# Talking-heads attention and gated convolution block: even chunks, wide first loads transposed by TensorE, first product a chunk later

## The chip, the cores and the metric

One core of one Trainium2 chip runs the whole program in one launch. The metric is the device time of a run in microseconds (us), as the median of a few runs; lower is better.

## The reference, cut to what matters

Four batches, 12 heads, 448 positions, 64 numbers a head, everything in fp32. Attention mixes its heads twice, before and after the softmax; a feed-forward block with a convolution over positions follows.

```
scores = 0.125 * q @ k.T                            # [4, 12, 448, 448]
scores = einsum('bhij,hg->bgij', scores, w_pre)     # heads mixed
attn   = softmax(scores)                            # exp(s - max) / (sum + 1e-9)
attn   = einsum('bhij,hg->bgij', attn, w_post)      # heads mixed again
x      = (attn @ v), heads side by side             # [4, 448, 768]
h      = relu(x @ w_in)                             # [4, 448, 1024]
c      = conv_w[0]*h[s-1] + conv_w[1]*h[s] + conv_w[2]*h[s+1]
out    = (h * sigmoid(c)) @ w_out                   # [4, 448, 768]
```

The weights of the feed-forward block come as 64-bit floats; the kernel loads them as pairs of 32-bit words and puts fp32 numbers together on the chip ("decoding": one ACT, one POOL and three DVE steps for a piece of 128x256).

## The kernel before, in words

The query rows of a batch are cut into tiles of 10 rows, and the tiles into four chunks: 9, 12, 12 and 12 tiles in batch 0, and 12, 12, 12 and 9 in the others (`TILES`, L27), so 16 chunks in all, numbered 0 to 15 here. A chunk goes through these steps:

- `qk` (L602): scores of two heads at a time, all rows of the chunk (90 or 120) against the 448 keys. A call is four matmuls on quarters of the array: for each of the two heads the first 64 rows and then the rest, 56 rows where the chunk has 120 and 26 where it has 90. Two copies (`qk_out`, ACT and DVE) bring the two heads from PSUM to SBUF. In chunk 0 the calls take turns between two PSUM pools, later all go through the two buffers of `ps_q`.
- `relayout` (L629): one DMA a head writes these rows into `mt`, where the 12 heads of one row lie on neighbouring partitions. There are two `mt` tiles, for odd and even chunks.
- `premix` (L638), a pair of tiles at a time: the first head mix on PE. Then row maximum (DVE), exponential with its sum (ACT), 1/sum (POOL, DVE), scaling of the second mix's weights by it (DVE), `postmix` (L685) on PE, whose result is already transposed (keys on partitions), and two copies to SBUF (`post_out`, ACT and DVE).
- `av` (L729): attention times v, two heads a call, six calls a chunk, and a copy into `x` (`av_out`).
- `mm1` (L780), per batch and 128 of the 1024 columns: x times w_in, six matmuls over the full array, then `relu` and a store to a scratch tensor in DRAM. For batches 0 to 2 two of these products stand in each chunk of the next batch; those of batch 3 come behind the last chunk.

In the end h is loaded again, convolved, gated and split in two parts (DVE, ACT), and `mm2` multiplies it by w_out in 672 matmuls.

The scores need q and k with their 64 numbers on partitions. Batch 0's keys and the queries of chunks 0 and 1 are loaded with rows on partitions (`load_k0`, `load_q0`) and transposed on PE with an identity matrix (`tr_k0`, `tr_q0`), then copied. All later queries and keys come in quarters: four DMAs of 32 partitions for one chunk's queries (`load_q`, L581) or for the keys of two heads (`load_k`, L567), and DVE transposes blocks of 32x32 (`tr_q`, `tr_k`). v of two heads comes in three DMAs in runs of 64 numbers, and POOL clears the rest of the last block.

The order of all instructions is fixed when the program is built: `plan` (L161) gives each operation an engine, a cost and a due time from a table `P` of numbers, and the class `Order` puts them in one list; each engine works through its part of it in order. Nearly all DMAs are issued by SP, in that order too: one whose data or buffer is not ready holds up those behind it.

Of the kernel before, what the change touches and what calls it, by code (L numbers as in the profile page):

```python
# [25 lines left out]
R, HR = 10, 5  # L26
TILES = [(9, 12, 12, 12)] + 3 * [(12, 12, 12, 9)]  # L27
# [18 lines left out]
T0, T1 = TILES[0][:2]  # L46
RH = R * (T0 + T1) // 2
ST_X = 6
N_PIECES = N_IN + FC * 3

P = dict(
    pm=-2.097, mx=-1.044, ex=-1.09, ep=-2.124, rc=0.122, wn=1.958, po=1.009, ev=0.636, qk=0.649, st=3.01,
    rl=-8.601, lead=6.642, av=2.442, ao=-0.878, a0=-3.11, q1w=0.882, q1s=-3.0, cw=1.318, vl=6.611, nq=5.578,
    nqs=-4.33, tq=14.316, ahead=17.24, tk=2.322, tks=0.913, nk=7.795, dec=14.624, dwi=3.76, dwo=5.594,
    wo0=108.805, look=0.033, step=2.1, busy0=5, k0a=-9.826, k0d=-0.402, m1=3.894, m1w=5.94, tail=4.022,
# [5 lines left out]
QUEUES = 8  # L61


class Order:


    def __init__(self):
        self.ops, self.done = {}, {}
# [5 lines left out]
    def run(self, free, look):  # L74
# [21 lines left out]
        rings, landed = [0.0] * 16, [0.0] * QUEUES  # L96
        shape = 1
        for _ in range(len(ops)):
# [19 lines left out]
            if isinstance(cost, tuple):  # L118
# [6 lines left out]
                end += .9  # L125
# [14 lines left out]
def q_rows(c):  # L140
    b, i0, T = CHUNKS[c]
    r0 = min(i0, S - 128) if c > 1 else i0
    return b, r0, i0 - r0
# [17 lines left out]
def plan(P):  # L161

    od = Order()

    def add(due, engine, cost, *key, after=(), ahead=None):
        od.add(due, engine, cost, *key, after=after, since=22 + (due - (ahead or P["ahead"])) * P["step"])
# [7 lines left out]
    for g in range(3):  # L174
        add(-11 + g, "PE", .55, "tr_q0", g, after=[("load_q0", g)])
        for c in range(2):
            add(-10.8 + g + 2 * c, ("DVE", "ACT")[c], (.3, .35)[c], "out_q0", g, c, after=[("tr_q0", g)])
    for p in range(NP):
        n = P["k0a"] + P["k0d"] * p
        add(n, "PE", .6, "tr_k0", p, after=[("load_k0", p), ("out_k0", p - 3)])  # L180
        add(n, ("ACT", "DVE")[p % 2], .5, "out_k0", p, after=[("tr_k0", p)])
# [3 lines left out]
    for c in range(NCH):  # L185
        if c >= 4:
            turns += [("mm1", c // 4 - 1, 2 * (c % 4) + i) for i in range(2)]
        turns += [("av", c, 0), ("av", c, 3)]

    order = []  # L190
    for x in turns:
        order.append(x)
    before = {}
    for x, y in zip(order, order[1:]):
        before[y] = ("relu", *x[1:]) if x[0] == "mm1" else ("av_out", *x[1:])
# [9 lines left out]
    for c in range(NCH):  # L205
# [33 lines left out]
        for h in range(H):  # L239
            n = sp - P["lead"] + h * w if c > 1 else P["q1s"] + P["q1w"] * h if c else -8.6 + .3 * h  # L240
            i = c * H + h
            free_s = [("qk_out", *divmod(i - 2 - j, H)) for j in range(2)]
            free_st = [("relayout", *slot_of[i])] if i in slot_of else []
            free_mt = [("premix", *pairs[number[c - 1, 0] - 1])] if h == 1 and c > 1 else []
            if h % 2:
                ops = [("tr_k", b, h // 2)] if b else [("out_k0", h // 2)]
                ops += [("tr_q", c, h // 6 * 3)] if c > 1 else [("out_q0", h // 4, c)]
                if c == 0:
                    ops += [("out_q0", g, 1) for g in range(min(h // 2 + 1, 3))]
                    free_s = [("qk_out", 0, h - 4 - j) for j in range(2)]  # L250
# [27 lines left out]
    for b in range(B):  # L278
        s0 = start_of(4 * b - 2)
        for p in range(NP):  # L280
            n = BASE[4 * b] + 1 + 2 * p + P["vl"] if b else 2.5 + p
            ready = [("av", 4 * b - 1, p)] if b else [("qk_out", 1, 5), ("relayout", 1, p)]
            for i in range(3):
                add(n + .1 * i, "SP", (.6, 16, .6) if i < 2 else (.4, 16, .2), "load_v1", b, p, i, after=ready)
            add(n, "POOL", .15, "zero_v", b, p, after=ready)
            add(n, "POOL", .0, "load_v", b, p, after=[("load_v1", b, p, i) for i in range(3)] + [("zero_v", b, p)])
            i = NP * b + p
            if b:
                n = s0 + P["tk"] + P["tks"] * (p - 2)
# [41 lines left out]
    for f in range(FC):  # L331
        if f < 3:
            free = [("premix", 14, len(PAIRS[14]) - 1)]
        elif f < 7:
            free = [("premix", last, len(PAIRS[last]) - 1)]
        else:
            free = [("tr_k", B - 1, NP - 1)]
# [42 lines left out]
    for g in range(3):  # L380
        od.done["load_q0", g] = 3.2 + 2.1 * g, "SP"
    for p in range(NP):
        od.done["load_k0", p] = 3.8 + .7 * p + .7 * (p // 2), "SP"
    order = od.run(dict(PE=4.0, ACT=4.2, DVE=2.0, POOL=9.0, SP=4.6), P["look"])
# [4 lines left out]
def tile_talking_heads_conv_glu(  # L389
# [48 lines left out]
    warm = const.tile([128, 1], F32, name="warm")  # L438
    wi = const.tile([128, KC, FF], U32, name="wi")
# [64 lines left out]
    def identity():  # L504
        nat["id"] = st_p.tile([128, 128], F32, tag="st", name="ident")
        make_identity(nc, nat["id"])

    def prepare():
# [434 lines left out]
```

## Time and profile before

| | us |
|---|---|
| median of 3 runs | 688.12 (685.66 to 689.55) |
| the profiled execution's own time | 690.48 |
| its span, first to last instruction | 688.7 |
| PE busy | 659.7 (96%) |
| DVE busy | 412.0 (60%) |
| ACT busy | 343.2 (50%) |

The mean granted TensorE clock is 0.977 of full speed. A record of PE includes time in which its matmul waits for others on the array, so the busy share of PE says little about how well it is used; what a piece of work takes is read from the start of one group of matmuls to the start of the next. A call of `qk` or a pair of tiles in `premix` shows as 8 records (each fp32 matmul is two), a pair of tiles in `postmix` as 64, three calls of `av` as 48, one `mm1` product as 12.

### The profile page before, as it was taken

To read this page: it belongs to the slowest core of one execution; us is meant where nothing else is said; L and a number is where in the kernel's file an instruction comes from. 1 tells how busy PE (TensorE), PEld (TensorE's weight loads), DVE (VectorE), ACT (ScalarE), POOL (GpSimd) and SP (SyncE) were. 2 spreads that over 40 slices of the span, in tenths; PEclk is the share of its full clock that TensorE was granted. 3 is DMA by queue.
4 is the path that set the end of the run, shared out by engine and by line. 5 is a ranking of instruction groups with operands and counts; after the bars stand their busy time and mean duration, and the time that the engine had idled before them with its cause. 6 is when DMAs were issued, how large, how long until landed. Compare 5 with 4: busy or idle time off the path is not lost.

```text
span 688.7 us, 23692 instructions
## 1 busy us (share of the span) xinstructions
PE 659.7 (96%) x9981; PEld 425.9 (62%) x9981; DVE 412.0 (60%) x974; ACT 343.2 (50%) x808; POOL 75.1 (11%) x186
## 2 busy tenths in 40 slices
PE   8899969799989999999999999999999999999997
PEld 6145646465635555645464655654565559999997
DVE  2467676775555666647474656644654399999100
ACT  3267645655545565646455565645634254434100
POOL 4000001231020220201100111101101000000000
PEclk9889988989999999999999999999999999999999
DMA  7766688878877658586755655632423443443111
GB/s 150 200 149 184 172 192 203 209 182 180 196 181 212 160 171 217 151 185 185 170 143 161 163 167 149 190 117 85 152 79 132 123 136 118 127 128 112 56 47 46
DMA packets 90348, 104.64 MB, mean 152 GB/s; under 512 B 32514, under 2 KB 79106, under 8 KB 90242
## 3 DMA queue, kind: packets, MB, share of 16 engines
q1 hardware_dynamic: 88846, 102.02, 55.3%
q8 instruction: 78, 1.28, 0.8%
q10 hardware_dynamic: 1299, 1.10, 0.6%
q14 instruction: 29, 0.23, 0.1%
q0 software_dynamic: 96, 0.01, 0.0%
HBM read 48.23 MB, written 15.99 MB: 93 GB/s over the span
## 4 chain that ended last, share of the span: by engine, by line
PE 85%; DMA 6%; ACT 3%; DVE 3%; issue 2%; SPq 1%; POOL 0%; ACTq 0%; DVEq 0%
PE h L784 21%; PE o L878 17%; PE s L614 14%; PE t L695 11%; PE a L736 10%; PE m L651 10%; DMA nq<-in_q_dram 2%; ACT e L664 1%; DMA nk<-in_k_dram 1%; DMA v<-in_v_dram 1%; DMA raw<-in_moe_w_in_dram 1%; PE tk L542 1%; ACT at L460 1%; DVE nm L656 1%; DVE mq L594 1%
## 5 line engine op out<-in xcount | busy, mean ns | idle before, releaser
L784 PE MATMUL h<-x,wi 128*128 128x448 f32 x384 | 159.1, 555 | 0.0
L664 ACT ACTIVATE e<-m,nm 124x448 f32<-124x448 f32 x180 | 114.9, 639 | 75.1 <-DVE nm L656 37.4
L656 DVE TENSOR_REDUCE nm<-m 124x1 f32<-124x448 f32 x180 | 106.4, 615 | 52.0 <-PE m L651 51.3
L695 PEld LDWEIGHTS t<-wn,e 60*64 60x64 f32 x5760 | 106.5, 137 | 47.8 <-issue 28.6
L614 PE MATMUL s<-mk,mq 64*64 64x448 f32 (+2 forms) x768 | 126.5, 577 | 7.4 <-ACT st L460 2.6
L460 ACT COPY st<-s 120x448 f32<-120x448 f32 (+1 forms) x161 | 82.1, 536 | 79.4 <-PE s L614 32.6
L878 PE MATMUL o<-wo,g 128*128 128x384 f32 x672 | 117.4, 337 | 0.0
L878 PEld LDWEIGHTS o<-wo,g 128*128 128x128 f32 x672 | 116.9, 188 | 0.4 <-DVE g L863 0.2
L695 PE MATMUL t<-wn,e 60*64 60x60 f32 x5760 | 110.6, 221 | 5.7 <-DVE at L462 2.4
L784 PEld LDWEIGHTS h<-x,wi 128*128 128x128 f32 x384 | 69.2, 191 | 75.0 <-issue 63.7
L651 PE MATMUL m<-mt,wpre 64*64 64x448 f32 (+1 forms) x704 | 96.5, 568 | 6.4 <-ACT e L664 3.0
L736 PEld LDWEIGHTS a<-at,v 128*64 128x64 f32 x1536 | 75.9, 139 | 22.9 <-issue 6.4
L736 PE MATMUL a<-at,v 128*64 128x120 f32 (+1 forms) x1536 | 86.3, 266 | 2.9 <-DVE at L462 0.9
L462 DVE COPY at<-t 128x480 f32<-128x480 f32 (+1 forms) x92 | 61.2, 666 | 31.8 <-PE t L695 31.4
L614 PEld LDWEIGHTS s<-mk,mq 64*64 64x64 f32 (+2 forms) x768 | 28.0, 131 | 63.3 <-issue 32.7
L460 ACT COPY at<-t 128x480 f32<-128x480 f32 (+1 forms) x92 | 57.9, 630 | 8.8 <-PE t L695 8.6
L670 POOL TENSOR_SCALAR sm<-sm 124x2 f32<-124x2 f32 (+1 forms) x92 | 21.4, 233 | 314.0 <-ACT e L664 308.0
L651 PEld LDWEIGHTS m<-mt,wpre 64*64 64x64 f32 (+1 forms) x704 | 25.3, 134 | 44.6 <-issue 30.3
L847 DVE SCALAR_TENSOR_TENSOR cv<-hpad,cws,cv 128x448 f32<-128x448 f32 x64 | 42.8, 678 | 0.1
L789 ACT ACTIVATE hs<-h 128x448 f32<-128x448 f32 x32 | 17.3, 542 | 47.5 <-PE h L784 34.5
L682 DVE TENSOR_SCALAR wn<-wpost,rs 124x60 f32<-124x60 f32 x180 | 37.0, 248 | 1.2
L664 ACT ACTIVATION_READ_ACCUMULATOR e<-m,nm 124x1 f32 x180 | 36.5, 203 | 0.0
(68 smaller groups left out, 377.8 us busy)
## 6 DMA issues: line engine op xcount, KB each, us to landing
mt<-st SPq DMA_DIRECT2D x120, 210.0 KB
nq<-in_q_dram SPq DMA_DIRECT2D x56, 168.0 KB
nk<-in_k_dram SPq DMA_DIRECT2D x72, 108.0 KB
mt<-st SPq DMA_DIRECT2D x48, 157.5 KB
h<-hs SPq DMA_DIRECT2D x32, 224.0 KB
hpad<-h SPq DMA_DIRECT2D x32, 224.0 KB
raw<-in_moe_w_in_dram SPq DMA_DIRECT2D x24, 256.0 KB
raw<-in_moe_w_out_dram SPq DMA_DIRECT2D x24, 256.0 KB
```

The source lines that it names most:

```text
L460: nc.scalar.copy(out=out, in_=in_)
L462: nc.vector.tensor_copy(out=out, in_=in_)
L614: nc.tensor.matmul(out=pqs[c, h - 1 + i][m:e], lhsT=qops[c][s, p, o + m:o + e], rhs=kops[b, p][s], start=True, stop=True)
L651: nc.tensor.matmul(out=pms[c, some[i]][64 * s:64 * s + 64], lhsT=wpre[rows, i], rhs=mt[rows, some[s]], start=True, stop=True)
L656: nc.vector.tensor_reduce(out=nm[0:PN], in_=pms[c, t][0:PN], axis=AX.X, op=ALU.max, negate=True)
L664: nc.scalar.activation(out=e[0:PN], in_=pms.pop((c, t))[0:PN], func=AF.Exp, bias=nm[0:PN], accum_out=sums[c, t // 2][0:PN, t % 2:t % 2 + 1])
L682: nc.vector.tensor_scalar(out=wns[c, k][0:PN, i], in0=wpost[0:PN], scalar1=rs[0:PN, i:i + 1], scalar2=None, op0=ALU.mult)
L695: nc.tensor.matmul(out=pts[c, k][s][64 * half:64 * half + 64, i, j], lhsT=e[rows, o:o + 64], rhs=wn[rows, i], start=True, stop=True)
L736: nc.tensor.matmul(out=pas[c][64 * hh:64 * hh + 64, p % 3, 0:n], lhsT=vts[b, p][:, hh, j, :], rhs=ats[c][:, j, 2 * p + hh, 0:n], start=(j ...
L784: nc.tensor.matmul(out=phs[b, f], lhsT=wi[:, kk, f * 128:(f + 1) * 128].bitcast(F32), rhs=xs[b][:, kk], start=(kk == 0), stop=(kk == KC - 1))
L847: nc.vector.scalar_tensor_tensor(out=cv, in0=hp[:, t:S + t], scalar=w, in1=cv, op0=ALU.mult, op1=ALU.add)
L878: nc.tensor.matmul(out=pos[r, o], lhsT=g, rhs=w, start=(f == 0 and j == 0), stop=(f == FC - 1 and j == 2))
```

## The change

1. The chunks of batch 0 have 10, 11, 12 and 12 tiles, those of the others 12, 12, 11 and 10. The number of tiles, of pairs of tiles and of `qk` calls stays.
2. Queries of chunks 0 to 7 are loaded with rows on partitions, in two DMAs of six heads a chunk (`q_load`), transposed on PE (`q_tr`, 12 matmuls for six heads) and copied by DVE or ACT (`q_out`). Keys of batches 0 and 1 go the same way (`k_load`, `k_tr`, `k_out`; 8 matmuls for two heads). The later ones take the old way. From chunk 2 and batch 1 on, these transposes use the two PSUM buffers of `qk`.
3. In batches 0 and 1 the keys stay in the order in which they were loaded (four neighbouring keys on a partition), so `k_out` copies straight, v of two heads is loaded in the same order by one DMA, `postmix` makes blocks of 64 and 48 keys, and `av` works on 112 partitions.
4. `mm1` of batches 0 and 1 stands one chunk later; batch 2's products are spread 3, 3 and 2 over the last three chunks.
5. At the start q of chunk 0 is loaded in two parts, keys between them; six of the 12 relayouts of chunk 0 are issued by ACT, and the clearing of `mt` by POOL instead of SP.
6. The numbers of the table `P` are others, and the order follows them.

```diff
-TILES = [(9, 12, 12, 12)] + 3 * [(12, 12, 12, 9)]
+TILES = [(10, 11, 12, 12)] + 3 * [(12, 12, 11, 10)]
+MM1_AT = [[4 * b + 5 + f // 2 for f in range(FC)] for b in range(B - 2)] + [[13, 13, 13, 14, 14, 14, 15, 15]]
+K_PE, Q_PE = 2, 8
...
-    nqs=-4.33, tq=14.316, ahead=17.24, tk=2.322, tks=0.913, nk=7.795, dec=14.624, dwi=3.76, dwo=5.594,
+    dec=15.218, dwi=5.977, dwo=5.863, wo0=107.878, look=0.04, step=0.16, step1=2.488, la=15.81, busy0=5,
...
+    def k_load(b, p, eng=nc.sync):
+        nat["k", b, p] = nat["k0"][:, p] if b == 0 else nk_p.tile([112, 2, JC, D], F32, tag="nk", name="nkr")
+        eng.dma_start(out=nat["k", b, p].rearrange("j h c d -> j h (c d)"),
+                      in_=k[b, 2 * p:2 * p + 2].rearrange("h (j c) d -> j h (c d)", c=JC))
+    def k_tr(b, p):
+        pl, tag = (ps_q, "s") if b else (ps_t, "t") if p % 3 < 2 else (ps_a, "a")
...
+    def k_out(b, p):
+        kops[b, p] = ko_p.tile([128, S], F32, tag="mk", name="mk")
+        copy_of(("ACT", "DVE")[p % 2], kops[b, p].rearrange("p (c j) -> p c j", c=JC), trs.pop(("k", b, p)))
+    def q_load(c, g, eng=nc.sync):
...
+        s = slice(6 * g, 6 * g + 6)
+        eng.dma_start(out=nat["q", c][:, s].rearrange("j n u d -> j n (u d)"),
+                      in_=q[b, s, r0:r0 + 128].rearrange("n (j u) d -> j n (u d)", u=2))
+    def q_tr(c, g):
+        pl, tag = (ps_m, "m") if c < 2 else (ps_q, "s")
+        ps = pl.tile([128, 3, 2, 64], F32, tag=tag, name="tq")
+        for p in range(3):
+            i = 6 * g + 2 * p
             for u in range(2):
                 for hh in range(2):
+                    nc.tensor.matmul(out=ps[64 * hh:64 * hh + 64, p, u], lhsT=nat["q", c][:, i + hh, u],
+                                     rhs=ident[0:64, 0:64], start=True, stop=True)
...
-        nc.sync.dma_start(out=nat["mt"][c % 2][4 + h:124:12, 0:T, :], in_=sts.pop((c, h))[0:R * T])
+        (nc.sync if c or h % 2 else nc.scalar).dma_start(out=nat["mt"][c % 2][4 + h:124:12, 0:T, :], in_=sts.pop((c, h))[0:R * T])
...
+    def blocks(c):
+        return 112 if CHUNKS[c][0] < K_PE else 128
...
-                o = min(128 * j + 64 * half, S - 64)
+                m = blocks(c) - 64 if half else 64
+                o = min(blocks(c) * j + 64 * half, S - m)
...
-        if i < 2:
+        if b < K_PE:
+            nc.sync.dma_start(out=vts[b, p][0:112].rearrange("j h c d -> j h (c d)"),
+                              in_=v[b, 2 * p:2 * p + 2].rearrange("h (j c) d -> j h (c d)", c=JC))
+        elif i < 2:
```

The first place is the start of PE's list. `tq` and `tk` are transposes of queries and keys, `s` are the scores (`qk`), `m` the first head mix. Before, from the second group of key transposes on:

```order
L542 MATMUL tk_256<-ident,nk_140 64x112 x8
L555 MATMUL tq_268<-ident,nq_141 64x105 x8
L542 MATMUL tk_279<-ident,nk_140 64x112 x8
L614 MATMUL s<-mk,mq 64x448 x2
L614 MATMUL s<-mk,mq 26x448 x2
L614 MATMUL s<-mk,mq 64x448 x2
L614 MATMUL s<-mk,mq 26x448 x2
```

And the changed program from its first transposes on:

```order
L613 MATMUL tq<-ident,nqr 64x64 x24
L587 MATMUL tk<-ident,nk_140 64x112 x16
L670 MATMUL s<-mk,mq 64x448 x2
L670 MATMUL s<-mk,mq 36x448 x2
L670 MATMUL s<-mk,mq 64x448 x2
L670 MATMUL s<-mk,mq 36x448 x2
L587 MATMUL tk<-ident,nk_140 64x112 x24
L670 MATMUL s<-mk,mq 64x448 x2
L670 MATMUL s<-mk,mq 36x448 x2
```

The rest of a chunk's rows is 36 (later 46 or 56) wide where it was 26. Ahead of the first `m` there are now nine calls of `qk`, four `q_tr` and six `k_tr`; before there were eleven calls, three `tr_q0` and six `tr_k0`.

The second place is SP's list of DMAs around the keys of batch 1 (`nk`, `nkr`); `mt` are relayouts, `raw` pieces of w_in, `nq`, `nqr` queries. Before:

```order
L586 DMA nq<-in_q_dram 32x6x224
L631 DMA mt<-stx 10x12x448 x2
L572 DMA nk<-in_k_dram 32x864 x4
L631 DMA mt<-stx 10x12x448
L765 DMA raw<-in_moe_w_in_dram 128x512
L572 DMA nk<-in_k_dram 32x864 x4
L631 DMA mt<-st 10x12x448
L586 DMA nq<-in_q_dram 32x6x224
L572 DMA nk<-in_k_dram 32x864 x4
L631 DMA mt<-st 10x12x448 x2
L765 DMA raw<-in_moe_w_in_dram 128x512
L572 DMA nk<-in_k_dram 32x864 x4
```

Changed, where the keys of batch 1 begin:

```order
L603 DMA nqr<-in_q_dram 64x6x128 x2
L578 DMA nkr<-in_k_dram 112x2x256 x2
L687 DMA mt<-stx 10x11x448 x2
L687 DMA mt<-stx 10x12x448 x3
L687 DMA mt<-st 10x12x448 x3
L830 DMA raw<-in_moe_w_in_dram 128x512 x3
L687 DMA mt<-stx 10x12x448 x4
L603 DMA nqr<-in_q_dram 64x6x128 x2
L687 DMA mt<-stx 10x12x448 x2
L830 DMA raw<-in_moe_w_in_dram 128x512 x2
L687 DMA mt<-st 10x12x448 x2
L578 DMA nkr<-in_k_dram 112x2x256
```

The keys of batch 1 began among the relayouts of chunk 3 and now begin at the end of those of chunk 1; two heads take one DMA instead of four, and a chunk's queries two instead of four.

## Rows read from the trace of the kernel before

**Rows 1.** Windows, seven stages: busy us (and instructions) of each engine, clock, DMA
```profile
0.00:35.38 35.38, 29.65 (x238) 13.99 (x242) 11.89 (x20) 10.56 (x18) 7.27 (x24) 0.91 0.72 176
35.38:73.62 38.24, 35.98 (x822) 20.13 (x814) 25.78 (x70) 28.06 (x73) 3.24 (x15) 0.95 0.67 163
73.62:142.83 69.21, 58.30 (x1306) 39.24 (x1304) 47.20 (x117) 37.40 (x94) 10.80 (x23) 0.88 0.84 198
142.83:173.10 30.27, 29.17 (x555) 16.09 (x553) 21.49 (x56) 18.59 (x48) 6.57 (x15) 1.00 0.76 179
173.10:270.07 96.97, 94.37 (x1583) 52.34 (x1583) 59.60 (x150) 53.57 (x133) 14.03 (x28) 0.98 0.71 186
270.07:532.00 261.93, 259.15 (x4721) 149.21 (x4721) 150.73 (x379) 146.29 (x357) 32.33 (x80) 1.00 0.54 151
532.00:688.70 156.70, 153.10 (x768) 134.94 (x768) 95.36 (x182) 48.74 (x89) 0.85 (x1) 1.00 0.31 98
```

**Rows 2.** Chain of waits, 78 to 100 us: start, us, what
```profile
78.75 2.93 DMA raw<-in_moe_w_in_dram
...
83.41 7.79 DMA nk<-in_k_dram
...
91.21 1.05 SPq L572
...
93.21 6.10 DMA nq<-in_q_dram
```

**Rows 3.** Timeline, 332 to 335 us, a call of `qk` on 90 rows
```profile
333.01 1.79 PE L614 MATMUL s<-mk,mq 64*64 64x448 f32 x8
...
333.87 0.13 PEld L614 LDWEIGHTS s<-mk,mq 64*26 64x26 f32 x4 [0.71 <-issue]
...
334.74 0.64 PE L784 MATMUL h<-x,wi 128*128 128x448 f32 x1
```

**Rows 4.** Timeline of PE, 275 to 277 us, a call of `qk` on 120 rows
```profile
275.27 0.93 PE L614 MATMUL s<-mk,mq 64*64 64x448 f32 x8
276.13 1.77 PE L784 MATMUL h<-x,wi 128*128 128x448 f32 x4
```

**Rows 5.** Groups by form, PE: mean ns of one record
```profile
L614 PE MATMUL s<-mk,mq 64*26 64x448 f32 x96 | 22.5, 545 | 0.0
```

**Rows 6.** Timeline of PE, 327 to 351 us: starts give the length of each piece
```profile
327.33 4.78 PE L784 MATMUL h<-x,wi 128*128 128x448 f32 x12
332.04 1.16 PE L695 MATMUL t<-wn,e 60*64 60x60 f32 x64
...
343.44 0.98 PE L651 MATMUL m<-mt,wpre 64*64 64x448 f32 x8
344.25 1.11 PE L695 MATMUL t<-wn,e 60*64 60x60 f32 x64
345.18 1.79 PE L614 MATMUL s<-mk,mq 64*64 64x448 f32 x8
...
347.81 2.68 PE L736 MATMUL a<-at,v 128*64 128x120 f32 x48
350.42 1.16 PE L695 MATMUL t<-wn,e 60*64 60x60 f32 x64
```

**Rows 7.** Chain of waits, 5 to 36 us, the start
```profile
5.23 1.67 PE tq L555 x16
...
9.21 0.72 PE tq L555 x16
...
11.70 2.45 PE tk L542 x48
...
15.64 8.88 PE s L614 x40
...
28.77 1.97 PE s L614 x6
30.73 0.52 ACT stx L460
```

More of the change, by code (lines that the diff above doesn't have):

```diff
@@ L89, in release @@
                     t = max(t, end + (LAG[e] if e != engine or e in ("SP", "DVE") else 0))
+                    if e == "SP" and engine != "SP" and "load" in k[0]:
+                        t = max(t, end + LAG[e] + self.late)
             ready[engine].append((due, i, t, key))
@@ L161, in plan, with add @@
 def plan(P):
-    od = Order()
-    def add(due, engine, cost, *key, after=(), ahead=None):
-        od.add(due, engine, cost, *key, after=after, since=22 + (due - (ahead or P["ahead"])) * P["step"])
+    od = Order(P["late"])
+    def add(due, engine, cost, *key, after=()):
+        x = due - (P["la"] if "load" in key[0] else P["ahead"])
+        od.add(due, engine, cost, *key, after=after, since=22 + P["step"] * min(x, 45) + P["step1"] * max(0, x - 45))
     last = NCH - 1
@@ L172, in plan, with k_ready, q_ready @@
     place = {x: i for i, x in enumerate(tiles)}
[L174 to L177, printed above, removed]
+    def k_ready(b, p):
+        return ("k_out" if b < K_PE else "tr_k", b, p)
+    def q_ready(c, h):
+        return ("q_out", c, h // 6) if c < Q_PE else ("tr_q", c, h // 6 * 3)
+    for c in range(2):
+        for g in range(2):
+            n = -11 + 2 * g if c == 0 else P["q1p"] + .3 * g
+            add(n, "PE", .55, "q_tr", c, g, after=[("q_load", c, g)] + [("k_tr", 0, 5)] * c)
+            add(n, ("DVE", "ACT")[g], .47, "q_out", c, g, after=[("q_tr", c, g)])
@@ L184, in plan @@
+    for x in seq:
+        if x[0] == "qk" and x[1] == 0 and x[2] % 4 == 3:
+            continue
+        outs = [("qk_out", x[1], x[2] - 1), ("qk_out", x[1], x[2])] if x[0] == "qk" else [(x[0][0] + "_out", *x[1:])]
+        free_s[x] = []
+        for o in outs:
+            free_s[x] += [banks[n_s % 2]] if n_s > 1 else []
+            banks[n_s % 2] = o
+            n_s += 1
+    for x, y in zip(seq, seq[1:]):
+        prev_s[y] = x
     turns = []
     for c in range(NCH):
-        if c >= 4:
-            turns += [("mm1", c // 4 - 1, 2 * (c % 4) + i) for i in range(2)]
+        turns += [("mm1", b, f) for b in range(B - 1) for f in range(FC) if MM1_AT[b][f] == c]
@@ L188, in plan @@
         turns += [("av", c, 0), ("av", c, 3)]
-    order = []
-    for x in turns:
-        order.append(x)
     before = {}
-    for x, y in zip(order, order[1:]):
+    for x, y in zip(turns, turns[1:]):
         before[y] = ("relu", *x[1:]) if x[0] == "mm1" else ("av_out", *x[1:])
@@ L378, in plan @@
         add(end + 14 + 4 * r + 6, "SP", (.4, 16, 1.0), "store", r, after=[("mm2_out", r, o) for o in range(2)])
[L380 to L384, printed above, removed]
+    for i, x in enumerate([("q_load", 0, 0)] + [("k_load", 0, p) for p in range(3)] + [("q_load", 0, 1)] + [
+            ("k_load", 0, p) for p in range(3, NP)] + [("q_load", 1, g) for g in range(2)]):
+        od.done[x] = 5.2 + i * .95, "SP"
+    order = od.run(dict(PE=4.0, ACT=4.2, DVE=2.0, POOL=10.0, SP=5.0), P["look"])
     return order, od
@@ L549, in tr_q0 @@
-    def tr_q0(g):
-        ps = ps_m.tile([128, 2, 2, RH], F32, tag="m", name="tq0")
-        for p in range(2):
-            i = 4 * g + 2 * p
+                nc.tensor.matmul(out=trs["k", b, p][64 * hh:64 * hh + 64, c], lhsT=x[:, hh, c],
+                                 rhs=ident[0:112, 0:112], start=True, stop=True)
+    def k_out(b, p):
+        kops[b, p] = ko_p.tile([128, S], F32, tag="mk", name="mk")
+        copy_of(("ACT", "DVE")[p % 2], kops[b, p].rearrange("p (c j) -> p c j", c=JC), trs.pop(("k", b, p)))
```

163 lines of the change are left out of this document (90 added, 73 removed).

## The prediction, made before the run

> **What bounds the kernel now.** I read the windows first, cut where the head mix of a chunk begins, so that each stage is a whole number of chunks [rows 1]: the start up to the first `premix`; chunks 0 and 1; chunks 2 and 3; chunk 4; chunks 5 to 7; chunks 8 to 15; the tail of `mm1` and `mm2`. The busy shares of PE do not tell much, so I price PE's work by the distance of starts at full clock [rows 4, 6]: a pair in `premix` 344.25 - 343.44 = 0.81 us, a pair in `postmix` 0.97 or 0.93, so 0.475 a tile, three `av` calls 350.42 - 347.81 = 2.61, so 0.87 each, an `mm1` product 332.04 - 327.33 = 4.71, a `qk` call on 120 rows 276.13 - 275.27 = 0.86. Counted from PE's list and priced so, chunks 0 and 1 hold 28.5 us of work in 38.2 us; chunks 2 and 3 hold 47.2 in 69.2; chunk 4 27.8 in 30.3; chunks 5 to 7 87.4 in 97.0; chunks 8 to 15 252.1 in 261.9. So from chunk 4 on PE sets the pace with some 4% to 10% lost, and the one big loss, 22 us, is in chunks 2 and 3. There the DMA engines are 84% busy at 198 GB/s, the highest of the seven stages, and the clock is at 0.88 [rows 1]: a mean of the two levels, 1.2 and 2.4 GHz, in a stretch where PE stands still. The chain names what comes late: a piece of w_in, then keys of batch 1 that take 7.79 us from issue to landing, then SP, then queries 6.10 us [rows 2].
>
> Inside PE's work there is a second loss. A `qk` call on 90 rows takes 334.74 - 333.01 = 1.73 us [rows 3], twice the 0.86 of one on 120 rows [rows 4], though it streams the same columns. Its 26-wide weight loads begin 0.86 us after the first matmuls and after 0.71 us of idle time: the second half of the call does not run beside the first. There are 96 such records [rows 5], 4 a call, so 24 calls: six in each of the four chunks of 90 rows.
>
> **The change part by part.** *No chunk of 90 rows.* PE's list has no 26-wide matmul left; the second halves are 36, 46 or 56 wide. 56 is fast by the rows, 26 slow; for 36 and 46 no row exists. Bounds: 0.86 or 1.73 us a call. I take 0.86, since half of a quarter-array fits them as it does 56. That takes 18 x 0.87 = 15.7 us off work on the path (six calls in chunks 5 to 7, twelve in 8 to 15) and 5.2 off the start.
>
> The Trainium skill bears on this ("TensorEngine Tiling (Array Packing)", section "Tiling Modes"): the array can be split into tiles, 64x64 and 64x32 among the forms, and a change of form drains it. By that rule 26 columns make a 64x32 form and 36 to 56 stay at 64x64, and the slow call of this trace agrees with it. It also speaks against the new key transposes, whose 112 rows need 128x64 among work in 64x64: 6 transposes x 2 changes x at most 0.44 (half of 0.87) would be 5 us on top of the sum below.
>
> *The start.* Before, PE goes from 5.23 to 15.64 us with transposes and one `qk` call, then five calls of chunk 0 in 8.88 us, then calls of chunk 1 about 2.5 us apart (28.77, copy at 30.73, next at 31.3) [rows 7], to the first `premix` at 35.4. Now both halves of chunk 0's queries are wanted first, and the second half is fifth among the loads. I estimate its landing at 9 us, from the first landing near 5.2 and, by the order of loads, about 0.95 us for each 0.2 MB at some 200 GB/s [rows 1, 7]. Then 2 key transposes (2.45 / 3 = 0.82 each), 2 `qk`, 3 + 1 transposes, 4 `qk`, two query transposes, and 3 `qk` calls of chunk 1 at about 1.6 (PE and a copy take turns on two buffers): 9 + 0.85 + 1.6 + a copy of 0.7 + 6 x 0.86 + 4 x 0.82 + 1.7 + 4.8 = 27.1, and 28 with the last relayout of chunk 0. Bounds 25 (loads land earlier) and 33 (the clock at its low level, as the 0.91 of this stage shows it before). The clearing of `mt` waits on POOL behind the weights, 7.27 us of work, and is covered until the first `premix`.
>
> *Transposes on PE.* A query transpose of six heads is 24 records of 64 columns where the known one is 16 of 105 in 0.72 us [rows 7]: by columns 0.66, by records 1.08; I take 0.85. After the start there are 12 of these and 6 for keys at 0.82: 10.2 + 4.9 = 15.1 us of new work, in chunks 0 to 7 only. They take buffers of `qk`, so a `qk` call behind one waits for its copy (0.52, [rows 7]); other PE work stands between in the list, which hides it, at most 18 x 0.5 = 9 us if not. DVE loses its block transposes and gets copies instead; with 47.20 of 69.21 us busy it is no bound [rows 1].
>
> *DMA.* A chunk's queries were 4 x 172 KB and are 2 x 197 KB; keys of two heads 4 x 111 KB, now one of 229 KB; v is the same in bytes, one issue for three. In chunks 2 and 3 DMA moved 198 x 69.2 = 13.7 MB. Without 3 x 0.29 MB of queries and 6 x 0.21 of keys it is 11.5 MB, 58.3 us at the same rate. Two things loosen it more: the keys of batch 1 start two chunks earlier, and w_in has one chunk more before `mm1`. One speaks against: three pairs of keys of batch 2 now come in before chunk 6.
>
> **The sum by stages**, PE's work counted from the new list:
> - Start: 28 (was 35.4).
> - Chunks 0 and 1: work 36.7, with 5 transposes and 3 `av` calls more. If it fills the 9.7 us lost before, the stage stays at 38.2; if the loss stays, 46.4. I take 42.5, about the middle: the losses are short waits in a chain from row maximum to copies, which extra PE work fills in part.
> - Chunks 2 and 3: work 50.7, which is the lower bound; the upper is 69.2 + 9 transposes, 76.7. I take the DMA's 58.3; the transposes are hidden beneath it.
> - Chunk 4, without `mm1`: work 23.6; with its 2.5 us of loss 26.
> - Chunks 5 to 7, four products instead of five and no slow call: 76.9, and the same 9.6 of loss, 86.5.
> - Chunks 8 to 15, 20 products instead of 17 (3 x 4.71 = 14.1 paid here), 12 slow calls less: 256.3 + 9.8 = 266.1.
> - Tail: 156.7 as before; its matmuls are the same, and DVE's convolutions begin behind the same decoding.
>
> Together 28 + 42.5 + 58.3 + 26 + 86.5 + 266.1 + 156.7 = 664.1 against a span of 688.7. The profiled run lies 1.8 us above its span and 2.4 above the median of the runs: 664.1 + 1.8 - 2.4 = 663.5, so 664 us, 3.5% less.
>
> **The rivals.**
> - *DMA stays the bound and the transposes come on top.* The stage of chunks 2 and 3 takes 76.7 and that of 0 and 1 46.4: 664 + 18.4 + 3.9 = 686, no change that shows. For it: SP works in order, and the chain goes from one late load to the next [rows 2]. Against: fewer bytes, fewer issues, earlier keys.
> - *PE stands behind a late load.* Before, a late key held up DVE; now the transpose itself is in PE's list, and `premix`, `postmix` and `av` wait behind it. The loads take 6 to 8 us when DMA is 84% busy [rows 1, 2]. It decides the sign from 24 / 18 = 1.3 us of wait for each of the 18 transposes on; with 2 us each it is 664 + 36 = 700, slower. Against: the earlier issue in SP's list, two chunks ahead of use.
> - *36 and 46 wide calls are slow as well.* Then 48 calls are slow instead of 24: 664 + 48 x 0.87 = 706. The fast 56 speaks against it [rows 4].
> - *The losses of chunks 0 to 4 all go*: 38.2, 50.7 and 23.6 there and 25 at the start, 664 - 17 = 647, and less if PE's steady loss of 4% shrinks. For it: the granted clock would be full all the time.
>
> **How the numbers follow.** The forecast has 0.66, the full gain 0.11, DMA as before 0.13, PE behind loads 0.06, slow narrow calls 0.04. The range runs from 645, just under the full gain, to 687, past the case of unchanged DMA, and leaves out the two slow cases and a better steady state. A change of 0.5% (3.4 us) is about what can be told from none: of the 0.13 I give half to faster, and so 0.85 for faster, 0.05 for no change, 0.10 for slower.
>
> **What would show it.** All `qk` calls at full clock 0.8 to 0.9 us apart, none at 1.7; first `premix` near 28 us; chunk 4's first `premix` near 129 and chunk 5's near 155 (were 142.8 and 173.1); a clock above 0.95 in chunks 2 and 3; the last `mm1` of batch 3 and all of `mm2` in 156 to 157 us. Wrong would be the forecast if PE shows waits for `nqr` or `nkr` of over 1 us in several places, if calls with 36 or 46 take 1.7 us, or if chunks 2 and 3 still take 69 us.

## The result, and the profile after

The changed kernel takes 676.2 us (675.3 to 676.9), the kernel before 687.1 in the same session: a ratio of 0.984 (0.980 to 0.987), some 11 us less. The sign was forecast, the size was not: the forecast had 24 us less. The profiled run after takes 676.86 us, 1.8 above its span.

First the windows of the changed kernel, cut as in [rows 1] at the first `premix` of the chunks. Columns: stretch, its length, busy us and instructions of PE, of PE's weight loads, of DVE, ACT and POOL, the granted clock, the busy share of the DMA engines, GB/s.

```profile
0.00:38.80 38.80, 25.61 (x269) 15.59 (x270) 9.04 (x16) 8.63 (x16) 7.99 (x23) 0.88 0.63 136
38.80:82.74 43.94, 42.00 (x1019) 28.08 (x1023) 29.41 (x79) 29.47 (x75) 5.42 (x14) 0.91 0.74 203
82.74:145.20 62.46, 56.12 (x1380) 39.48 (x1376) 43.97 (x117) 39.78 (x101) 12.69 (x23) 0.95 0.69 181
145.20:171.60 26.40, 24.63 (x648) 16.94 (x643) 18.23 (x48) 18.54 (x46) 3.86 (x9) 1.00 0.62 174
171.60:252.84 81.24, 80.64 (x1559) 48.32 (x1558) 53.19 (x132) 50.41 (x127) 8.20 (x22) 1.00 0.76 181
252.84:518.35 265.51, 261.24 (x4793) 157.67 (x4785) 156.94 (x401) 149.80 (x366) 36.25 (x85) 1.00 0.58 161
518.35:675.10 156.75, 153.21 (x770) 135.05 (x768) 97.00 (x173) 47.31 (x87) 0.00 (x0) 1.00 0.28 90
```

Against the sum's terms, in us:

| stage | before | forecast | after | after - forecast |
|---|---|---|---|---|
| start | 35.4 | 28 | 38.8 | +10.8 |
| chunks 0, 1 | 38.2 | 42.5 | 43.9 | +1.4 |
| chunks 2, 3 | 69.2 | 58.3 | 62.5 | +4.2 |
| chunk 4 | 30.3 | 26 | 26.4 | +0.4 |
| chunks 5 to 7 | 97.0 | 86.5 | 81.2 | -5.3 |
| chunks 8 to 15 | 261.9 | 266.1 | 265.5 | -0.6 |
| tail | 156.7 | 156.7 | 156.7 | 0 |

The sum is 11.0 above the forecast, and the start alone 10.8. Up to chunk 4 nothing is won: its first `premix` comes at 145.2 us, where it came at 142.8. The gain of the profiles lies behind it: 15.7 us in chunks 5 to 7 and 3.9 in chunk 4, of which chunks 8 to 15, with three products more, give 3.6 back.

The chain of waits of the changed kernel, 0 to 39 us, shows where the start goes (start, length, what):

```profile
2.26 7.82 DMA nqr<-in_q_dram
...
10.13 1.54 PE tq L613 x24
11.67 3.18 PE tk L587 x32
14.86 1.36 PE s L670 x4
...
16.76 1.40 ACTq L687
...
18.76 4.47 ACTq L687
23.23 0.04 issue
23.27 0.54 ACT mk L510
...
33.01 5.66 DMA mt<-st
38.67 0.14 issue
38.80 1.77 PE m L707 x8
```

ACT stands still for 4.47 us while it issues one relayout (L687), and its copies, on which the next `qk` calls wait, stand behind it. The instructions of `mt` up to 40 us, by engine (ns min/median/max), show that this was one issue of six, that SP had such a one too (5.30 us), and what else was under way:

```profile
L687 ACTq DMA_DIRECT2D mt<-st x6: 785/786/4471, 16.8 to 33.0; - x6
L687 SPq DMA_DIRECT2D mt<-st x6: 755/756/5296, 16.9 to 32.8; - x6
...
L565 POOL DMA_DIRECT2D mt<-zero x2: 597/636/675, 14.0 to 14.6; - x2
```

POOL issues the clearing of `mt` at 14.0 and 14.6 us, and the DMA view gives it a median of 10.8 us to landing. Meanwhile DMA moves next to nothing (windows of the changed kernel):

```profile
18.00:20.00 2.00, 1.33 (x28) 1.12 (x24) 0.62 (x1) 0.53 (x1) 0.00 (x0) 1.00 0.85 65
20.00:22.00 2.00, 0.00 (x0) 0.00 (x0) 0.00 (x0) 0.00 (x0) 0.00 (x0) 1.00 0.28 25
22.00:24.00 2.00, 0.14 (x4) 0.14 (x8) 0.00 (x0) 0.73 (x2) 0.00 (x0) 0.60 0.41 56
24.00:26.00 2.00, 2.00 (x12) 0.69 (x16) 0.28 (x1) 0.56 (x2) 0.00 (x0) 0.50 0.57 181
```

25 to 65 GB/s from 18 to 24 us, where the stage's mean is 136; PE does nothing from 20 to 22, and the granted clock then falls to its low level, 1.2 GHz.

The calls of `qk` came out as forecast. On 100 rows, the second halves 36 wide (by-form lines of one call of chunk 11, then the timeline of PE):

```profile
L670 PE MATMUL s<-mk,mq x8: 534/537/542, 336.5 to 336.9; 64*64 64x448 f32 x4, 64*36 64x448 f32 x4
```

```profile
336.46 0.93 PE L670 MATMUL s<-mk,mq 64*64 64x448 f32 x8
337.22 0.93 PE L707 MATMUL m<-mt,wpre 64*64 64x448 f32 x8
```

0.76 us from start to start, where a call on 90 rows took 1.73 [rows 3]; one with 46-wide halves at 304.7 takes 0.75.

### The profile page after: what moved, and what is told of

The parts are those of the page before. It is cut to its first block, busy times and chain, and to the rows that moved or that the text cites. A ratio compares the mean times of both kernels' runs of the same rounds, so it can differ in the third digit from the quotient of the medians.

```text
span 675.1 us, 24446 instructions
## 1 busy us (share of the span) xinstructions
PE 643.4 (95%) x10413; PEld 441.1 (65%) x10413; DVE 407.8 (60%) x964; ACT 343.9 (51%) x816; POOL 74.4 (11%) x176
## 3 DMA queue, kind: packets, MB, share of 16 engines
q8 instruction: 82, 1.34, 0.9%
## 4 chain that ended last, share of the span: by engine, by line
PE 88%; DMA 5%; ACT 2%; issue 2%; DVE 1%; ACTq 1%; SPq 1%; POOL 0%; DVEq 0%
PE h L849 22%; PE o L943 17%; PE a L801 12%; PE t L756 12%; PE m L707 11%; PE s L670 11%; DMA mt<-st 2%; PE tq L613 2%; PE tk L587 1%; DMA nqr<-in_q_dram 1%; ACTq L687 1%; DMA nk<-in_k_dram 1%; ACT st L510 1%; DMA mt<-stx 1%; DMA v<-in_v_dram 1%
## 5 line engine op out<-in xcount | busy, mean ns | idle before, releaser
L756 PEld LDWEIGHTS t<-wn,e 60*64 60x64 f32 (+1 forms) x5760 | 104.9, 131 | 47.2 <-issue 28.3
L510 ACT COPY st<-s 120x448 f32<-120x448 f32 (+2 forms) x161 | 82.4, 538 | 77.5 <-DMA mt<-st 38.6
L756 PE MATMUL t<-wn,e 60*64 60x60 f32 (+1 forms) x5760 | 109.3, 218 | 4.9 <-DVE at L512 1.7
L670 PE MATMUL s<-mk,mq 64*64 64x448 f32 (+3 forms) x768 | 103.8, 571 | 7.9 <-ACT mk L510 4.5
L512 DVE COPY at<-t 128x480 f32<-128x480 f32 (+3 forms) x92 | 61.4, 667 | 49.6 <-PE t L756 49.2
L801 PE MATMUL a<-at,v 112*64 112x120 f32 (+5 forms) x1536 | 86.8, 266 | 4.0 <-ACT at L510 1.8
L801 PEld LDWEIGHTS a<-at,v 112*64 112x64 f32 (+1 forms) x1536 | 75.6, 139 | 21.9 <-issue 6.6
L510 ACT COPY at<-t 128x480 f32<-128x480 f32 (+3 forms) x92 | 58.3, 634 | 17.4 <-PE t L756 17.1
L670 PEld LDWEIGHTS s<-mk,mq 64*64 64x64 f32 (+3 forms) x768 | 27.2, 130 | 38.4 <-issue 14.0
L915 ACT ACTIVATE cv<-cv 128x448 f32<-128x448 f32 x32 | 18.5, 578 | 39.2 <-DVE cv L912 39.0
```

The lines of the kernel that those rows point to most:

```text
L510: nc.scalar.copy(out=out, in_=in_)
L512: nc.vector.tensor_copy(out=out, in_=in_)
L670: nc.tensor.matmul(out=pqs[c, h - 1 + i][m:e], lhsT=qops[c][s, p, o + m:o + e], rhs=kops[b, p][s], start=True, stop=True)
L756: nc.tensor.matmul(out=pts[c, k][s][64 * half:64 * half + m, i, j], lhsT=e[rows, o:o + m], rhs=wn[rows, i], start=True, stop=True)
L801: nc.tensor.matmul(out=pas[c][64 * hh:64 * hh + 64, p % 3, 0:n], lhsT=vts[b, p][0:m, hh, j, :], rhs=ats[c][0:m, j, 2 * p + hh, 0:n], start ...
```

## The experiments

All edits are made to the changed kernel, except e1 and e9. Ratios are to the kernel before, measured in the same session (684.0 to 687.1 us). e3, e5, e12 and e13 leave PE's and DVE's order as it is in the changed kernel (e12 adds matmuls to PE's), e9 leaves the order of before; the others make the planner write a new one.

**e3: SP issues the clearing of `mt`.**

```
-        nc.gpsimd.dma_start(out=nat["mt"][i][0:4],
+        nc.sync.dma_start(out=nat["mt"][i][0:4],
...
```

> The changed kernel with the two DMAs that clear four partitions of mt issued by SP behind the first loads, as before, instead of by POOL. Theory 'POOL's DMA': the 4.5 and 5.3 us that ACT and SP stand at their second relayouts from 18 to 23 us are due to the clearing DMAs, which take 10.8 us from 14 us on; without them the first premix comes at 31 to 34 us instead of 38.8 and the time is 670 to 673 us. Rival 'two queues': relayouts issued by ACT and SP at once hold each other up; then the stand at 18 us stays, first premix at 38 to 40, time 675 to 678 us.

674.1 us, ratio 0.981 (0.975 to 0.987). The first `premix` comes at 32.17 us, 6.6 earlier, and the long issues are gone:

```profile
L687 ACTq DMA_DIRECT2D mt<-st x6: 785/786/1392, 16.3 to 26.3; - x6
...
L565 SPq DMA_DIRECT2D mt<-zero x2: 682/756/829, 5.9 to 9.3; - x2
```

So the clearing as POOL issued it made the long issues and the 6.6 us. The edit moves two things at once, the issuer and the moment (from 14.0 to 5.9 us), and no run has SP clear at 14 us or POOL at 6. The DMA packets in the kept traces speak for the issuer: POOL's two transfers went as 32 packets of 5,376 bytes, which took 0.2 to 5.9 us each, 1.8 in the median, between 15.2 and 24.5 us; SP's went in packets of 1,792 bytes, 0.28 us in the median, from 10.8 us on.

The time falls by only some 2 us, 0.981 against 0.984, which the intervals don't tell from nothing: chunks 0 and 1 take 48.2 us instead of 43.9. PE stands still there for 2.65 us in chunk 0's `av` (below), and behind that the clock is low for some 3.4 us (0.79 in the mean of 54 to 62 us), worth some 1.7 us: 4.3 together, where the stage is 4.2 longer.

**e4: the relayouts of chunk 0 all on SP, POOL clears.**

```
-        (nc.sync if c or h % 2 else nc.scalar).dma_start(...
+        nc.sync.dma_start(...
```

> The changed kernel with all 12 relayouts of chunk 0 issued by SP; the clearing stays with POOL. Theory 'POOL's DMA': a relayout issue still stands for about 5 us near 18 us, now on SP alone, PE's keys are no longer held up by ACT; first premix 37 to 40 us, 674 to 678 us. Rival 'two queues': no issue over 2 us near 18 us, first premix 31 to 35 us, 669 to 673 us.

679.4 us, 0.990 (0.987 to 0.993). One issue of SP still takes 4.53 us (14 issues, 755/756/4527 ns). With ACT out of it, PE is not held, but the first `premix` waits for a relayout and comes at 39.2. Two issuing engines are not the cause, since one alone has the long issue too; what is left is POOL's transfer. The time lies above both expectations (674 to 678 and 669 to 673), with an order that the planner wrote anew.

**e5 and e13: as e3, and both halves of chunk 0's queries loaded ahead of the keys.**

```
-        ... ((q_load, 0, 0, 0), (k_load, 0, 0, 1), (k_load, 0, 1, 0), (k_load, 0, 2, 1), (q_load, 0, 1, 0),
+        ... ((q_load, 0, 0, 0), (q_load, 0, 1, 1), (k_load, 0, 0, 0), (k_load, 0, 1, 1), (k_load, 0, 2, 0),
```

> The changed kernel with SP clearing `mt` (as in e3) and with both halves of chunk 0's queries loaded before all keys, one by SP and one by ACT. The second half then lands near 7 us instead of 10.1, so the first `premix` should start 2 to 3 us before the 32.2 us of e3, at 29 to 30, by either theory. Theory 'chunks 0 and 1 take it back' (in e3 a first `premix` 6.6 us earlier left only 2.4 us at chunk 2's first `premix`, 80.3 against 82.7): chunk 2 begins at 79 to 80.5 again and the time is that of e3, 672 to 675 us. Rival 'an earlier start is kept': chunk 2 begins at 77 to 78, and the time falls by the same 2 to 3 us, to 670 to 672.

> The kernel of e5 again, with more runs, beside e12 on the same chip: by every theory 667 to 671 us, chunk 2's first `premix` at 75 to 77.

669.8 us, 0.976 (0.970 to 0.982); again, 671.3 us, 0.978 (0.973 to 0.984). The first `premix` comes at 29.5 and 29.9. The time fell as the rival of e5 has it: the earlier start is kept, in part. This version is faster than the kernel before, and by the ratios some 4 to 5.5 us faster than the changed kernel, in both runs, though the intervals touch; its start is 9 us shorter. Its windows (e5, cut at the same five places as the first five above):

```profile
0.00:29.54 29.54, 21.59 (x269) 14.03 (x270) 9.05 (x16) 8.63 (x16) 6.77 (x21) 0.98 0.73 177
29.54:75.83 46.29, 43.30 (x1019) 28.67 (x1022) 29.41 (x79) 29.37 (x75) 5.42 (x14) 0.90 0.74 194
75.83:134.37 58.54, 52.69 (x1380) 37.89 (x1376) 43.91 (x117) 40.18 (x101) 12.40 (x23) 1.00 0.70 191
134.37:160.29 25.92, 24.04 (x644) 16.68 (x640) 18.19 (x48) 18.45 (x46) 3.86 (x9) 1.00 0.68 185
160.29:241.35 81.06, 80.47 (x1558) 48.06 (x1552) 53.24 (x132) 50.78 (x127) 8.20 (x22) 1.00 0.75 180
```

But one profile is one execution. In the profile of e13 (678.5 us; its other runs 668.7 to 672.5) chunk 2 begins at 81.8 instead of 75.8, with the same program. The six us begin with a stand, idle time of PE, in chunk 0's `av`, which is 2.9 us longer in e13; most of the rest comes right behind it, where the clock is at its low level. Windows of e13, then of e5:

```profile
54.00:62.00 8.00, 7.15 (x80) 5.88 (x84) 1.20 (x3) 0.00 (x0) 0.00 (x0) 0.50 0.64 174
```

```profile
54.00:62.00 8.00, 8.00 (x118) 5.05 (x118) 3.95 (x10) 3.29 (x10) 0.21 (x1) 0.89 0.69 175
```

80 matmuls start in e13's eight us and 118 in e5's. So this stand cost twice, once as a wait and once as a low clock behind it. The stands of PE in e3, e5, e13, and then e12 (timelines; the bracket holds the idle time before):

```profile
56.06 3.64 PE L801 MATMUL a<-at,v 112*64 112x100 f32 x44 [2.65 <-issue]
```

```profile
51.52 3.25 PE L801 MATMUL a<-at,v 112*64 112x100 f32 x44 [0.95 <-issue]
```

```profile
54.85 3.94 PE L801 MATMUL a<-at,v 112*64 112x100 f32 x44 [3.84 <-issue]
```

```profile
49.88 0.74 PE L670 MATMUL s<-mk,mq 64*56 64x448 f32 x2 [2.57 <-issue]
...
55.75 0.41 PE L756 MATMUL t<-wn,e 60*48 60x60 f32 x12 [0.75 <-issue]
```

"issue" means that no semaphore was waited for. The windows up to the stand count what PE had done by then, in e13 and in e12:

```profile
0.00:54.50 54.50, 42.71 (x729) 27.32 (x729) 22.54 (x50) 22.80 (x51) 7.86 (x26) 0.93 0.78 190
```

```profile
0.00:55.40 55.40, 44.25 (x729) 28.53 (x730) 21.62 (x49) 22.32 (x50) 7.86 (x26) 0.97 0.78 187
```

729 matmuls in e3, e5 and e13; and 729 in e12 too, where 16 matmuls more stand ahead of that place and the stand falls in other work. e12's stand that ends at 49.88 comes after 602 matmuls, and e3, e5, e12 and e13 all have one after 2632. The distances are 127 and 1903 = 15 x 126.9, with as many weight loads. The DMA queue "q8 instruction", which carries instructions, moves 82 packets in 1.34 MB in the whole run, 16.3 KB each; 20,826 matmuls and loads of PE are 82 times 254. So a block is 254 of PE's instructions, and the stand is PE's next block that has not come. The times of the packets in the kept traces agree. The stands after 602, 729 and 2632 matmuls fall to the queue's 4th, 5th and 20th packet, and in all four runs each ends 1.3 to 1.8 us after its packet has landed: in e13 the 5th packet is under way from 52.03 to 53.39 us, and PE goes on at 54.85. In the changed kernel the 5th packet lands at 58.14, before PE needs it, and there is no such stand there.

The Trainium skill ("Runtime: NRT & Kernel Launch", section "Instruction fetch mechanics") has the fetch in blocks of 16 KiB or 256 instructions by DMA, at a cost that is mostly hidden: the packets agree with the block; that it is hidden doesn't hold here in chunk 0, 0.95 to 3.84 us in one program. The packet itself is not long, 0.9 to 1.4 us, but it begins late, from 1.6 us before PE runs out to 1.0 us after. What holds it back is not shown; the busy DMA (79% of it at 48 to 58 us in e5) is likely, and was not tried by itself.

**e12: e5 with matmuls on zeros in the stands of the start.**

```
+        fill = {("qk", 1, 3): 3, ("qk", 1, 5): 3, ("premix", 0, 0): 10}
...
+            if (name, *a) in fill:
+                keep_busy(fill[(name, *a)], ps_t)
```

> The kernel of e5 with 16 more matmuls on zeros, which nothing reads: three ahead of each of two `qk` calls of chunk 1, ten ahead of the first `premix`, where PE stood 0.8, 0.6 and 2.3 us in e5; everything else in e5's order. In e5 the granted clock was 0.55 and 0.60 from 28 to 36 us, and a pair in `premix` and a transpose of queries there took about twice their time. Theory 'the stand costs twice, once as a wait and once as a low clock behind it': the clock is above 0.9 from 28 to 36, the first `premix` stays at 29 to 30, chunk 2's first `premix` comes 2 to 4 us earlier than the 75.8 of e5, and the time falls to 666 to 668. Rival 'what is lost in chunks 0 and 1 is waits for transfers': chunk 2 begins at 75 to 76 whatever the clock, and the time is 669 to 671.

669.7 us, 0.976 (0.971 to 0.981), against e13's 671.3 in the same session: not to be told apart. The clock did what was expected. Windows from 28 to 36 us of e13, then of e12:

```profile
28.00:32.00 4.00, 2.12 (x20) 1.26 (x22) 0.31 (x1) 0.00 (x0) 0.00 (x0) 0.74 0.68 233
32.00:36.00 4.00, 4.00 (x34) 2.30 (x32) 2.58 (x6) 1.63 (x5) 0.23 (x1) 0.50 1.03 260
```

```profile
28.00:32.00 4.00, 3.02 (x22) 2.21 (x20) 0.62 (x1) 0.54 (x1) 0.00 (x0) 1.00 0.61 213
32.00:36.00 4.00, 3.45 (x46) 1.46 (x40) 2.87 (x7) 1.76 (x5) 0.23 (x1) 1.00 0.83 239
```

46 matmuls start in four us instead of 34. But the fill put the first `premix` 1.5 us later (31.3), and chunk 2 begins at 81.5, where the theory had 72 to 74 and the rival 75 to 76. This profile (675.8 us, where the median is 669.7) has the stands of 2.57 and 0.75 us at late blocks and a low clock behind them, so it says nothing on what the fill gained. The time is in the rival's 669 to 671, but so is e13's, or nearly: e12 decides neither way.

**e9: the kernel before in its own order, 12 of 24 narrow calls made wide.**

```
+                if n == 90 and m and c and p % 3 < 2:
+                    e = 100
+                    lhsT = qops[c].rearrange("d p j -> d (p j)")[s, 128 * p + o + m:128 * p + o + e]
...
```

> The kernel before, in its own order on every engine, with one edit: in the chunks of 90 rows of batches 1 to 3 (7, 11 and 15), in the four of six `qk` calls where the next pair's queries lie behind, the second half streams with 36 columns instead of 26 (ten rows of PSUM more, which nothing reads). 12 of the 24 slow calls become wide; nothing else moves. Theory 'a narrow call costs 0.87 us of PE's path': 12 x 0.87 = 10.4 us less, 675 to 678 us where the kernel before has 686, and e1 lost its gain to a disturbed order. Rival 'the narrow calls are mostly hidden': 682 to 686, about what e1 gave for all 24.

678.4 us, 0.990 (0.985 to 0.995): 7.1 us less (3.7 to 10.4), 0.6 a call and up to the 0.87 of the theory. Timeline of PE, two wide calls and one left narrow in the same chunk:

```profile
318.04 0.93 PE L618 MATMUL s<-mk,mq 64*64 64x448 f32 x8
318.90 4.78 PE L787 MATMUL h<-x,wi 128*128 128x448 f32 x12
...
324.59 0.93 PE L618 MATMUL s<-mk,mq 64*64 64x448 f32 x8
325.45 1.02 PE L787 MATMUL h<-x,wi 128*128 128x448 f32 x2
...
329.94 1.84 PE L618 MATMUL s<-mk,mq 64*64 64x448 f32 x8
331.71 2.52 PE L787 MATMUL h<-x,wi 128*128 128x448 f32 x6
```

0.86, 0.86 and 1.77 us: ten columns more make the call half as long.

**e1 and e2: the tiles alone.** e1 is the kernel before with the new `TILES`, e2 the changed kernel with the old.

```
-TILES = [(9, 12, 12, 12)] + 3 * [(12, 12, 12, 9)]
+TILES = [(10, 11, 12, 12)] + 3 * [(12, 12, 11, 10)]
```

> The kernel before with only the new chunk sizes (10, 11, 12, 12 and 12, 12, 11, 10 tiles); all loads and transposes as before. Theory 'narrow calls': the 24 calls of qk that took 1.73 us take 0.86, so 15.7 us less on the path and up to 5 us less in the start: 687 - 16 to 687 - 21, 666 to 671 us. Rival 'the gain of the change comes from the loads': within 3 us of before, 684 to 690 us. In the trace no qk call at full clock lasts 1.7 us under the first theory also where 36 or 46 rows are left.

> The changed kernel with the old chunk sizes (9, 12, 12, 12 and 12, 12, 12, 9 tiles); new loads, transposes on PE and later first product stay. Theory 'narrow calls': 676 + 16 to 21 = 692 to 697 us, slower than before, so that the other parts together cost time. Rival: 676 to 680 us, the loads carry the gain.

e1: 680.3 us, 0.992 (0.989 to 0.995), 6 less instead of 16 to 21. e2: 698.5, 1.015 (1.006 to 1.024), by the ratios 21 above the changed kernel. One is far below the price of the calls, the other near it; e10 and e11 show what may blur them.

**e10 and e11: another order of the same operations.** One constant of the planner 0.1 higher (`wn=7.302`, and `av=3.403`).

> The changed kernel with one constant of the planner (`wn`, the due time of a copy) 0.1 higher, and so the same operations in another order on each engine, no other edit. It sizes what a new order alone does. Theory 'an order that the constants were not chosen for costs much': 682 us or more, so that the 22 us of e2, the 12 of e7 and the 8 of e8 hold a good part that is order alone. Rival 'order alone costs little': 674 to 679, and those differences stand as measured.

> As the run before it, with another constant (`av`) 0.1 higher: a second order of the same operations. Theory: 682 us or more; rival: 674 to 679.

678.4 us, 0.989 (0.985 to 0.993), and 680.9, 0.992 (0.989 to 0.995): 0.5% and 0.8% above the changed kernel, some 3.5 and 5.5 us by the ratios. Order alone thus costs less than the theory's 682, but not nothing. Of e2's 21 us that much may be order, which leaves 16 to 18 for the calls, where the forecast had 15.7 + 5.2 = 20.9. In e1 a new order as bad as that, 3 to 6 us, would explain a part of what is missing; the rest stays open. The price of a call rests on e9, where the order does not change.

**e6: as e3, w_in loaded later.**

```
-            after=free + [("relayout", 1, min(i, 3) + 6), ("qk_out", 1, 9)])
+            after=free + [("relayout", 1, min(i, 3) + 6), ("qk", 2, 11)])
```

> The changed kernel with SP clearing `mt`, and no piece of w_in is loaded before the last `qk` call of chunk 2 has been issued. In e3 some 6 pieces of 0.256 MB come between 55 and 83 us. Theory 'the loads pulled ahead hold up chunks 0 and 1': 1.5 MB less at some 190 GB/s frees up to 8 us of the DMA engines, chunks 0 and 1 go from 48.1 us to 43 to 45, and chunks 2 and 3 get longer than 62.0; the time stays within 2 us of e3 (672 to 676), or more if the first products at chunk 5 stand. Rival 'chunks 0 and 1 are a chain of short waits that no load makes': they stay at 47 to 49 us.

674.0 us, 0.985 (0.979 to 0.992). First `premix` at 32.1, that of chunk 2 at 80.5: 48.4 us for chunks 0 and 1, as e3's 48.2. The rival holds: the loads pulled ahead do not make that stage long.

**e7: keys of batch 1 and queries of chunks 2 to 7 loaded and transposed as before.** `K_PE` also puts batch 1's v and its blocks of keys back as they were.

```
-K_PE, Q_PE = 2, 8
+K_PE, Q_PE = 1, 2
```

> The changed kernel with only the first batch's keys and the first two chunks' queries loaded wide; keys of batch 1 and queries of chunks 2 to 7 come in quarters as before and are transposed by DVE. 18 transposes (about 15 us of PE) go, 3.1 MB of padded loads and DVE's transposes come back. Theory 'the wide loads pay through the DMA stage': chunks 2 and 3 go from 62.5 to 67 to 71 us, chunks 4 to 7 get 3 to 6 us shorter, time 676 to 684. Rival 'the transposes cost more than the bytes': chunks 2 and 3 stay at 60 to 63, and the time is 664 to 672.

688.4 us, 1.006 (1.002 to 1.010), 2.2% or 15 us worse than the changed kernel. Both expectations missed: the time is above either. Even with 3 to 6 us taken off for order, wide loads with transposes on PE are the better way, by more than the theory had. But not by the theory's path: chunks 2 and 3 take 62.9 us, as in the changed kernel (62.5). Chunks 4 to 7, which were to get shorter, take 126.6 instead of 107.6, of which two products more in that stretch are 9.4. Why the rest is lost there stays open.

**e8: the first products as early as before.**

```
-MM1_AT = [[4 * b + 5 + f // 2 for f in range(FC)] for b in range(B - 2)] + [[13, 13, 13, 14, 14, 14, 15, 15]]
+MM1_AT = [[4 * b + 4 + f // 2 for f in range(FC)] for b in range(B - 1)]
```

> The changed kernel with the first products in the chunks they had before (from chunk 4 on), the rest as changed. Theory 'the work is only moved': chunk 4 goes up by 2 products (9.4 us), chunks 8 to 15 down by three (14 us), chunks 5 to 7 by one up, and the time is 674 to 680. Rival 'the later product is what gives w_in the time': PE stands for w_in in chunks 2 to 4 as the kernel before did (22 us lost in chunks 2 and 3), and the time is 683 or more.

683.8 us, 0.996 (0.992 to 1.000), 8 us worse than the changed kernel. The time is the rival's (683 or more), but PE does not stand for w_in in chunks 2 to 4, so the rival's mechanism fails; 4.1 us of the difference lie in chunks 0 and 1 (48.1 for 43.9), ahead of any product, and 3 to 6 us may be order. What the later product is worth stays open.

## Why the prediction was wrong, and where it was right

- **The start failed**: "The clearing of `mt` waits on POOL behind the weights, 7.27 us of work, and is covered until the first `premix`", and with it the 28 us. I priced the clearing at nothing, as work on POOL, not as a transfer that other engines' relayouts run into. Measured: 38.8 us, of which the clearing as POOL issued it makes 6.6 (e3: 32.2) and the second half of the queries, fifth among the loads, 2.6 (e5: 29.5); it landed at 10.1, where I had 9. What is left over the 28 is 1.5 us. My upper bound, 33, took a slow clock for the worst and left the queues out. Of the 9.3 us that e5 takes off the start, the time keeps some 4 to 5.5 (e5, e13).
- **The narrow calls held**: fast at 36 and 46 wide, and in e9, whose order is that of before, worth 0.3 to 0.87 us each. The sign of the forecast rests on the chunk sizes: without them the changed kernel is slower than before (e2, 1.015).
- **Chunks 5 to 7 came out better than the sum, by 5.3 us**: 81.2 for 86.5. The work was 76.9 as counted, so the loss is 4.3 us and not the 9.6 that I carried over from before: PE's idle time fell from 2.6 to 0.6 us, and the clock rose from 0.98 to 1.00. The sum had no reason for this, so it is luck, and it hides 5.3 us of what the other terms missed.
- **Chunks 2 and 3**: 62.5 for 58.3. The bytes were right, 181 x 62.46 = 11.3 MB for 11.5, but DMA is 69% busy and not the bound I took it for. In the changed kernel PE waits 1.9 us for a copy at 113, and the clock of the eight us from 114 on is 0.79; in e5 the stage takes 58.5 at a full clock (timeline and windows of the changed kernel, then windows of e5, behind that place):

```profile
113.12 0.97 PE L670 MATMUL s<-mk,mq 64*64 64x448 f32 x6 [1.94 <-ACT st L510]
```

```profile
114.00:122.00 8.00, 7.44 (x87) 4.78 (x88) 3.23 (x8) 2.76 (x7) 0.22 (x1) 0.79 0.80 192
```

```profile
106.00:112.00 6.00, 5.89 (x88) 3.96 (x92) 3.24 (x8) 2.93 (x8) 0.22 (x1) 1.00 0.91 229
```

  So where the number was near, it was for a wrong reason, and that is luck. Since e13's profile gives 62 again, a few us here are one execution's.
- **Key transposes**: the 5 us that a change of form might have cost did not show. Among other work they take 0.82 to 0.91 us from start to start, where the sum had 0.82; the longest, in the changed kernel:

```profile
90.94 0.99 PE L587 MATMUL tk<-ident,nkr 112*64 112x112 f32 x16
91.85 0.85 PE L613 MATMUL tq<-ident,nqr 64*64 64x64 f32 x21
```

- **Chunks 0 and 1**: 43.9 for 42.5, near, but not by the short waits that I had left over: in the changed kernel PE is idle for 1.9 us only, and the mean clock is 0.91, worth some 4 us. In e5 the stage takes 46.3, with a clock of 0.90 and a stand of 0.95 us at a late block of instructions. The sum had no term for a low clock behind a stand nor for a late block.
- **Chunks 8 to 15** held: they lost 265.5 - 256.3 = 9.2 us where I carried over 9.8.
- **The rivals.** DMA as the bound would have shown 84% busy again; it shows 69%. PE behind late loads: waits for `nqr` come to 4.9 us in two places, both at the start, none for `nkr`. With the start mended (e5) 664 becomes 670 to 671. In e5's profile chunks 0 and 1 are 3.8 us above the forecast, chunks 8 to 15 3.9 above, the start 1.5 above, and chunks 5 to 7 5.4 below.

## What to carry to other kernels

A transfer is not covered because its engine has time: ask what shares the DMA engines with it while it lands. A smaller matmul can cost more than a larger one, as calls with 26 columns did against those with 36 to 56: look at start distances, not at record durations (545 ns for the slow ones [rows 5], 537 in the fast call above). Before a one-constant change is given credit for a few us, run the same operations in another order, and the same program twice.

## What the runs showed of the hardware that was not expected

- While two transfers of 84 KB issued by POOL were under way (10.8 us to landing), single issues on ACT and SP took 4.47 and 5.30 us instead of 0.79 and 0.76, and DMA moved 22 to 65 GB/s from 16 to 24 us; issued by SP at 5.9 to 9.3 us they did no such thing. The Trainium skill ("DMA: Bandwidth & Descriptors", section "Issuing engines are not separate DMA queues") lets DMAs of all engines interleave on the same 16 engines, whichever engine started them. I read that as saying that the issuer should not matter much; here the change of issuer and moment together was worth 6.6 us of the start, and the packets were cut differently.
- PE stands still at blocks of about 254 instructions, up to 3.84 us, if the next block is late, and works at a low clock after the long ones (0.50 from 54 to 62 us in e13).
- A call whose second half is 26 columns wide takes 1.77 us; with 36, 46 or 56 it takes 0.75 to 0.9.
